# An RWKV scan followed by a soft mixture of experts: first loads on another queue, a split last weight, and a new order of all tasks

## The chip, the cores and the metric

The kernel runs on one core of a Trainium2 chip. The metric is the device time of one execution in microseconds (us), as the median of several runs. A profiled execution gives the times of the single instructions. In this text PE is TensorE, DVE VectorE, ACT ScalarE, POOL GpSimd and SP the engine that only issues transfers. A transfer is issued on the queue of one engine and is carried out by 16 DMA engines.

## What is computed

The reference is an RWKV-5 recurrence whose output goes through a soft mixture of experts:

```python
for t in range(S):                       # B=4, H=8, S=768, D=48
    cur = einsum('bhd,bhe->bhde', u * k[t], v[t])
    y[:, :, t] = einsum('bhd,bhde->bhe', r[t], state + cur)
    state = w * state + einsum('bhd,bhe->bhde', k[t], v[t])
x = y as (3072, 384)
logits = x @ phi                         # phi (384, 32): 8 experts of 4 slots
d = softmax of logits over the 3072 rows;  slot_input = d.T @ x
for e in range(8):                       # w1 (8, 384, 1024), w2 (8, 1024, 384)
    slot_out[e] = relu(slot_input[e] @ w1[e]) @ w2[e]
c = softmax of logits over the 32 slots;  out = c @ slot_out
```

The inputs k, r, v are 14.2 MB of f32, the weights w1 and w2 25.2 MB, the output 4.7 MB.

## The kernel before

The recurrence is cut into chunks of 128 times for two batches at once: 12 steps n, of which two share a load unit U (0 to 5). A unit has six loads (k, r, v for two batches x = 0, 1), each of 128 rows of 3072 bytes; the transfer casts f32 to bf16. They are issued on POOL (`load`, L333). For each unit PE transposes them (L447), DVE multiplies k and r by decay tables while it evicts (L458), ACT evicts v (L455). `pr` (L471, on POOL from unit 1 on) is the product of k and r. In step n PE turns k and v back (L485), forms A = k r (L512), which DVE masks (L517); it forms the state sums (L543, L547; evicted by ACT, L554; scaled to Z by POOL, L557) and y (L580 to L587), where DVE makes the diagonal term dv (L563). ACT evicts y to x (L594); x is transposed (L609, L612), and multiplied with phi (L628) into logits.

`combine(U)` makes the softmax over the slots (its last product on POOL, L664), `dispatch(g)` the slot inputs of four groups of steps, `finish_slots` folds them. `first_layer` (L863 to L889) has 4 experts side by side, each in 32 of the 128 output rows, for two groups g of four experts; its hidden units are transposed back (L886, L889) to hT. `second_layer` (L905) multiplies hT with w2: 64 products of 384 columns that all add into one bank `SO`, 4 experts side by side. One ACT instruction scales SO into `so` (L910). `output` forms 24 row groups of the output (L934), evicted in turn by DVE and ACT (L936, L938), and stores them by eight transfers of 1, 2, 3, 4, 4, 4, 4, 2 groups on SP (L940).

The weights are 16 transfers of 768 KB (as bf16) on POOL: w1 of 8 experts (L847), w2 of 8 experts (L850). w2 goes into the space that raw inputs had.

The order of the work is not that of the source. Every piece is a `task` with a priority, an engine, an estimated duration, what it reads and writes, and the buffers it uses. `Plan.order` simulates the engines, and chooses by time and by priority; the table TUNE shifts priorities of single tasks. `Plan.emit` then writes the instructions in that order, and puts filler matmuls on PE (L922) where the plan has gaps before the first A and after the last y. Each engine works strictly through its own list; waits for data are added by the framework. The list of POOL matters below: it holds pr, Z, the softmax products, and the issue of all transfers of inputs and weights.

At the start, DVE clears buffers, SP and ACT load w and u (four transfers of 1.5 KB, `wu`), SP loads phi, POOL issues k, and only then makes the identity matrix. PE clears eight banks (L387), and then transposes `wu` (L399), from which come the logarithms (L402) and the decay tables (L407, L410).

Of the kernel before, what the change touches and what calls it, by code (L numbers as in the profile page):

```python
# [11 lines left out]
class Plan:  # L12
# [4 lines left out]
    def __init__(self, tune):  # L17

        self.tune = tune
        self.tasks, self.pools, self.writers, self.readers, self.users = [], {}, {}, {}, {}  # L20
        self.slot, self.landed = {}, []
# [30 lines left out]
    def order(self):  # L52
# [9 lines left out]
        while ready:  # L62
            best = None
            for i in ready:
# [51 lines left out]
        return [i for _, _, i in sorted(out)]  # L116

    def emit(self, where, fill, took=0.22):
# [11 lines left out]
TUNE = {46: (0.6, 0.0), 47: (-0.81, 0.2), 48: (-0.47, 0.0), 49: (1.82, 0.0), 50: (-0.25, 0.2), 73: (-2.02, 0.0),   # L130
# [82 lines left out]
def kernel(  # L213
# [176 lines left out]
    for b_ in banks:  # L390
        task(-150, "PE", 0.4, lambda b_=b_: clear(b_), r=["warm"], w=["cleared"], n=1)
# [557 lines left out]
    for e in range(E):  # L949
        load_w(e, True)  # L950
# [41 lines left out]
```

## Time and profile before

| what | value |
|---|---|
| median of 3 runs | 119.11 us (118.87 to 119.14) |
| the profiled execution's own time | 118.71 us |
| its span, first to last instruction | 116.9 us |
| granted TensorE clock | 0.973 |
| busy: PE, DVE, ACT, POOL | 99.7, 92.9, 78.4, 72.6 us |
| HBM read, written | 39.38 MB, 4.72 MB |

How to read it: the profile's durations are of one profiled execution, whose own time is 1.8 us longer than its span. A row of the timeline gives start, duration (of the first start to the last end where there are several), engine, line, operation, output and input, and count; in brackets stands what the engine waited for before. PEld is the load of weights into the array. POOL's rows `DMA_DIRECT2D` are its time for issuing a transfer; SPq and ACTq are issues on those queues. A row of the stretches gives, after the stretch, its length, the busy time and the number of instructions of PE, PEld, DVE, ACT and POOL, the granted clock, the share of the DMA engines' time that was busy, and the GB/s that they wrote.

### The profile page before, as it was taken

The page shows a single profiled execution, that of the slowest core. Times are in us where ns is not written, and L with a number is a line of the kernel's source. Part 1 is how long each engine was busy: PE and PEld are TensorE (multiplying, and loading weights), DVE is VectorE, ACT ScalarE, POOL GpSimd, SP SyncE. Part 2 cuts the span into 40 slices and gives each one's busy share as a digit, 9 for nine tenths or more (in the row PEclk, how much of TensorE's full clock was granted, in tenths as well). Part 3 has the DMA queues.
Part 4 walks back from the last instruction along what each step waited for, and adds up shares of the span by engine and source line. Part 5 has one row for each costly group of instructions (what it writes and reads, how often), then busy time and mean ns, then how long its engine had stood idle before and what let it go on. Part 6 is the DMA issues. An engine that isn't in the chain of part 4 may idle for free.

```text
span 116.9 us, 4280 instructions
## 1 busy us (share of the span) xinstructions
PE 99.7 (85%) x1844; PEld 71.7 (61%) x1844; DVE 92.9 (80%) x152; ACT 78.4 (67%) x159; POOL 72.6 (62%) x111
## 2 busy tenths in 40 slices
PE   5979999999998999999989998999899995655200
PEld 1354587778786788777868777787665552445100
DVE  6789599999999999999999899999975561086400
ACT  4261878788789697895888898889764750175400
POOL 6999848999999999894769945999111010000000
PEclk9999999999999999999999999999999999999955
DMA  2999999999999999999999999999999994059994
GB/s 10 171 187 198 208 206 205 209 205 209 206 207 209 230 209 212 223 210 221 214 208 224 210 220 210 214 219 216 208 219 216 210 219 98 0 196 410 419 421 170
DMA packets 9122, 24.70 MB, mean 211 GB/s; under 512 B 1424, under 2 KB 6160, under 8 KB 9104
## 3 DMA queue, kind: packets, MB, share of 16 engines
q0 software_dynamic: 7488, 19.66, 87.2%
q1 hardware_dynamic: 1584, 4.77, 10.4%
q8 instruction: 14, 0.23, 0.7%
q14 instruction: 4, 0.03, 0.1%
q10 hardware_dynamic: 32, 0.00, 0.0%
HBM read 39.38 MB, written 4.72 MB: 377 GB/s over the span
## 4 chain that ended last, share of the span: by engine, by line
PE 32%; POOL 27%; DMA 24%; issue 4%; DVE 4%; ACT 2%; DVEq 0%; POOLq 0%
DMA raw<-in_moe_w_dram 17%; POOL raw L339 12%; PE T L447 8%; POOL arena L471 7%; DMA raw<-in_k_dram 7%; POOL Z L557 5%; PE T L485 5%; PE Ab L512 3%; DVE arena L936 3%; PE Y L580 2%; PE T L609 2%; ACT arena L938 2%; PE Y L587 1%; PE Sb L531 1%; PE Y L585 1%
## 5 line engine op out<-in xcount | busy, mean ns | idle before, releaser
L458 DVE TENSOR_TENSOR arena<-T,tab 128x1024 bf16<-128x1024 bf16 x24 | 29.0, 1217 | 2.5 <-PE T L447 2.2
L517 DVE TENSOR_TENSOR arena<-Ab,mask 128x1024 bf16<-128x1024 f32 x24 | 29.2, 1216 | 0.9 <-PE Ab L512 0.8
L447 PE MATMUL T<-by_head,raw 128*48 128x128 bf16 x576 | 22.8, 221 | 1.2 <-DMA raw<-in_r_dram 0.7
L471 POOL TENSOR_TENSOR arena<-arena 128x1024 bf16<-128x1024 bf16 x10 | 21.4, 2136 | 0.6 <-DVE arena L458 0.5
L447 PEld LDWEIGHTS <-raw 128*48 128x48 bf16 x576 | 16.9, 102 | 6.4 <-issue 3.3
L557 POOL TENSOR_TENSOR Z<-Ss,wCm 128x384 bf16<-128x384 f32 x20 | 16.7, 841 | 5.1 <-ACT Ss L554 5.0
L455 ACT COPY arena<-T 128x1024 bf16<-128x1024 bf16 x12 | 12.2, 1017 | 3.7 <-PE T L447 3.5
L594 ACT CAST x_all<-Y 128x384 bf16<-128x384 f32 x23 | 11.1, 489 | 1.6 <-PE Y L587 1.5
L485 PE MATMUL T<-ident,arena 112*128 112x112 bf16 x176 | 12.0, 213 | 0.1
L554 ACT COPY Ss<-Y 128x384 f32<-128x384 f32 x20 | 9.7, 491 | 3.0 <-PE Y L547 2.7
L563 DVE TENSOR_TENSOR dv<-vn,Sb 128x768 bf16<-128x768 bf16 x12 | 11.3, 946 | 0.2
L489 ACT COPY vn<-T 128x768 bf16<-128x768 bf16 x12 | 9.7, 811 | 2.4 <-PE T L485 2.2
L612 ACT COPY xT<-T 128x768 bf16<-128x768 bf16 (+2 forms) x13 | 9.7, 758 | 1.3 <-PE T L609 1.0
L485 PEld LDWEIGHTS <-arena 112*128 112x128 bf16 x176 | 9.3, 97 | 1.5 <-DVE arena L458 0.3
L512 PE MATMUL Ab<-arena 48*128 48x128 bf16 x192 | 9.7, 219 | 0.3 <-issue 0.3
L664 POOL TENSOR_TENSOR Le<-E,rs 128x128 bf16<-128x128 f32 x6 | 2.4, 400 | 11.5 <-PE Ab L863 5.9
L580 PE MATMUL Y<-vn,arena 128*128 128x48 bf16 x192 | 8.8, 184 | 0.2 <-DVE arena L517 0.2
L489 ACT COPY kn<-T 128x768 bf16<-128x768 bf16 x10 | 8.0, 805 | 0.8 <-PE T L485 0.7
L339 POOL DMA_DIRECT2D raw<-in_k_dram x12 | 6.5, 554 | 2.4 <-DMA raw<-in_v_dram 1.4
L587 PE MATMUL Y<-dv,ident 128*128 128x384 bf16 x24 | 7.8, 325 | 0.0
L580 PEld LDWEIGHTS <-arena 128*128 128x128 bf16 x192 | 6.8, 96 | 1.4 <-DVE arena L517 0.3
L512 PEld LDWEIGHTS <-arena 48*128 48x128 bf16 x192 | 5.5, 94 | 3.1 <-issue 1.6
(146 smaller groups left out, 197.9 us busy)
## 6 DMA issues: line engine op xcount, KB each, us to landing
w_all<-in_moe_w_dram POOLq DMA_DIRECT2D x8, 768.0 KB, 17.7
raw<-in_moe_w_dram POOLq DMA_DIRECT2D x8, 768.0 KB, 20.6
out_dram<-arena SPq DMA_DIRECT2D x4, 768.0 KB, 5.6
raw<-in_k_dram POOLq DMA_DIRECT2D x12, 192.0 KB, 6.9
raw<-in_r_dram POOLq DMA_DIRECT2D x12, 192.0 KB, 7.0
raw<-in_v_dram POOLq DMA_DIRECT2D x12, 192.0 KB, 7.2
out_dram<-arena SPq DMA_DIRECT2D x2, 384.0 KB, 2.4
out_dram<-arena SPq DMA_DIRECT2D x1, 576.0 KB, 2.9
```

The source lines that it names most:

```text
L339: pool.dma_start(out=raw_of(which, U, x), in_=ap)), w=[("raw", 6 * U + 2 * which + x)], dma=0.97, lag=7)
L447: O(pe.transpose(T[64 * x:64 * x + D, C * j:C * j + C], raw_of(which, U, x)[:, jj * D:(jj + 1) * D], by_head[:]))
L455: O(act.copy(dst, src))
L458: O(dve.tensor_mul(dst.rearrange("p j (h c) q -> p j h c q", c=2), src.rearrange("p j (h c) q -> p j h c q", c=2), tb[:, :, :, None, :].to ...
L471: O((pool if U else dve).tensor_mul(pr_t[P["pr", 2 * U + b]].rearrange("p (h a) -> p h a", h=H), kt, rt))
L485: O(pe.transpose(T[:, h * C:h * C + 64 + D], cell(st[P[src, U]], h, cc)[0:64 + D], ident[0:64 + D, 0:64 + D]))
L489: O(act.copy(nt[P[name, n]][:].rearrange("p h x d -> p (h x) d")[:, :, 0:D], T[:].rearrange("p (a d) -> p a d", d=64)[:, :, 0:D]))
L512: O(pe.matmul(Ab[:, x, i * C:(i + 1) * C], cell(kt, 4 * rd + i, cc)[s], cell(rt, 4 * rd + i, cc)[s], start=True, stop=True))
L517: O(dve.tensor_mul(AT[:, :, 4 * rd:4 * rd + 4, :], Ab[:].rearrange("p x (h t) -> p x h t", h=4), mask[:, None, None, :].to_broadcast([128, ...
L557: task(n + 0.2 + 0.05 * hh, "POOL", 0.8, lambda hh=hh: O(pool.tensor_mul(Z_t[P["Z", (n, hh)]][:], Ss_t[P["Ss", (n, hh)]][:], wCm[:, 4 * hh ...
L563: O(eng.tensor_mul(dv_t[P["dv", n]][:].rearrange("p h x d -> p (h x) d"), vn_t[P["vn", n]][:].rearrange("p h x d -> p (h x) d"), sums[:, : ...
L580: O(pe.matmul(Y[:, (2 * i + x) * D:(2 * i + x + 1) * D], AT[:, x, h, :], vn[:, h, x, :], start=(i == 0 and x == 0), stop=False, skip_group ...
```

## The change

- **First loads.** The two k transfers of unit 0 are issued on SP, as f32 without a cast, into the space of the AT ring; one ACT copy each casts them to bf16. w and u on SP follow the first of them, phi the second. POOL issues r first, and makes the identity between its first two loads.
- **phi.** phi is read as `(p mo) s` and not `(mo p) s`, so each of 128 rows is 384 bytes long and no longer three rows of 128 bytes. The transposition of x therefore takes every third column (`mi:Dm:nM`).
- **Clears.** Of the clears, the transposition of `wu` waits only for that of its own bank (in SEQ it comes fourth on PE, after three clears); two warm-up matmuls instead of six.
- **Last weight.** w2 of expert 7 comes in two transfers, of 6 and of 2 of its 8 row blocks y. The experts 3 and 7 (the last of each group) leave SO: they add into two banks of their own, halves of 192 columns. The scaling into `so` is three instructions: ACT for 96 rows of 384 columns, and, for the last 32 rows, ACT and DVE for 192 columns each.
- **Output.** Nine transfers of 1, 1, 1, 2, 3, 4, 4, 4, 4 groups. The first group is formed and evicted in two halves, by ACT and DVE.
- **Step 11.** The first part of its x transposed is evicted by DVE instead of ACT, and its transposition waits for all of x.
- **Order.** TUNE is gone. A list SEQ of all 613 tasks sets the order of every engine.

POOL's own list, from SEQ, in names (it holds no transfer outside this list but k of unit 0):

```
r U0 x0, identity, r U0 x1, identity, iota, v U0, k U1 x0, ucol, k U1 x1, r U1, v U1, k U2, ...
... w1 6, pr n6, pr n7, Z n6, Le U0, w1 7, Z n6, w2 0, phi4, w2 1, Z n7, pr n8, Ed U1, Z n7, pr n9,
w2 2, Z n8, Z n8, Ed U2, Z n9, pr n10, Z n9, Le U1, Le U2, pr n11, phi4, w2 3, Ed U3, w2 4, w2 5,
Z n10, Z n10, phi4, w2 6, Le U3, Le U4, Le U5, w2 7 (6 blocks), w2 7 (2 blocks)
```

PE's list ends, after the last transposition of x and the slot inputs, with the first layer, then

```
hT g0 b1, hT g0 b0, h g1 a0, rest 0 x1, hT g1 b0, hT g1 b1,
most 0, rest 0 x0, most 1, most 2, most 3, rest 1 x0, rest 1 x1, rest 2 x1, rest 2 x0
```

DVE's list around the end of the recurrence is: ev r U5 b1, dv n9, AT n9, rs U1, rs U2 and their reciprocals, AT n10, dv n10, AT n10, rm U3, cm g1, AT n11, dv n11, AT n11 (ev is L458, AT L517).

```diff
-    def __init__(self, tune):
-        self.tune = tune
+    def __init__(self, tune, seq=()):
+        self.tune, self.seq = tune, seq
...
-            for i in ready:
+            if self.seq:
+                i = self.seq[len(out)]
...
+            for i in () if self.seq else ready:
...
-        return [i for _, _, i in sorted(out)]
+        return list(self.seq) or [i for _, _, i in sorted(out)]
...
+        if i == 0:
+            for x in (at,):
+                st = AT_t[x].bitcast(f32)[:, 0:JD]
+                task(-220, "SP", 1.7 - 0.8 * x, lambda x=x, st=st: O(sp.dma_start(out=st, in_=aps[x])), r=["sp"], w=[("st", x), "sp"])
+                task(-98, "ACT", 0.75, lambda x=x, st=st: O(act.copy(raw_of(0, 0, x), st)), r=[("st", x)], w=[("raw", x)])
...
-    banks = [t[:].bitcast(f32) for t in T_b] + [Ab[:, 0, :], Ab[:, 1, :], Y_b[0][:], Y_b[1][:], Sb[:]]
+    banks = [Sb[:]] + [t[:].bitcast(f32) for t in T_b] + [Ab[:, 0, :], Ab[:, 1, :], Y_b[0][:], Y_b[1][:]]
...
-    warm_up(6, -94, r=["cleared"])
+    warm_up(2, -94, r=["cleared1"])
...
-                        O(pe.transpose(T[:, o:o + C], xx[:, x, mi * C:(mi + 1) * C], ident[:]))
+                        O(pe.transpose(T[:, o:o + C], xx[:, x, mi:Dm:nM], ident[:]))
...
+            y0, y1 = (0, nF) if e < E - 1 else (YL if part else 0, nF if part else YL)
+            more = dict(w=[("w2", e, 1)], behind=w2_first[e]) if part else dict(
+                w=[("w2", e, 0)] + [("raw", 4 * e + i) for i in range(4)])
+            w2_first.setdefault(e, task(-40 + e + 10 * part, "POOL", 0.57, lambda: O(pool.dma_start(
+                out=w2_of(e)[:, y0:y1], in_=moe_w2[e].rearrange("(p y) d -> p y d", p=128)[:, y0:y1])),
+                dma=3.7 * (y1 - y0) / nF, lag=lag, **more))
...
+        lk = [("Y", "so0"), ("Y", "so1")]
+        EL, DH, RL = EG - 1, Dm // 2, 32 * (EG - 1)
+        def most(g, y0, y1):
+            for y in range(y0, y1):
+                for j in range(EL):
+                    O(pe.matmul(SO[32 * j:32 * j + 32, :], hT[g][:, y, 32 * j:32 * j + 32], w2_of(g * EG + j)[:, y, :],
+                                start=(g == 0 and y == 0), stop=(g == 1 and y == nF - 1), skip_group_check=True))
+        def rest(g, y0, y1, x):
+            s = slice(x * DH, (x + 1) * DH)
+            for y in range(y0, y1):
+                O(pe.matmul(Y_b[P[lk[x]]][RL:128, 0:DH], hT[g][:, y, RL:128], w2_of(g * EG + EL)[:, y, s],
+                            start=(g == 0 and y == 0), stop=(g == 1 and y == nF - 1), skip_group_check=True))
+        for q, (g, y0, y1) in enumerate(((0, 0, YH), (0, YH, nF), (1, 0, YH), (1, YH, nF))):
...
+        for q, (g, y0, y1) in enumerate(((0, 0, nF), (1, 0, YL), (1, YL, nF))):
...
+        task(80, "ACT", 0.55, lambda: O(act.mul(so[0:RL, :], SO[0:RL, :], rcs[0:RL, 0:1])), r=["SO", "rcs"], w=["so"], use=key)
+        task(81, "ACT", 0.35, lambda: O(act.mul(so[RL:128, 0:DH], Y_b[P[lk[0]]][RL:128, 0:DH], rcs[RL:128, 0:1])),
...
+        task(81, "DVE", 0.35, lambda: O(dve.tensor_scalar(
+            out=so[RL:128, DH:Dm], in0=Y_b[P[lk[1]]][RL:128, 0:DH], scalar1=rcs[RL:128, 0:1], scalar2=None, op0=ALU.mult)),
...
-        for sz in (1, 2, 3, 4, 4, 4, 4, 2):
+        for sz in (1, 1, 1, 2, 3, 4, 4, 4, 4):
...
+                for x, cp in enumerate((act.copy, dve.tensor_copy)):
+                    s = slice(x * Dm // 2, (x + 1) * Dm // 2)
+                    O(pe.matmul(ob[x][:, s], LexpT[:, 0:Nn:nN], so[:, s], start=True, stop=True))
+                    O(cp(obuf[:, 0, s], ob[x][:, s]))
```

More of the change, by code (lines that the diff above doesn't have):

```diff
@@ L63, in order @@
             best = None
-            for i in ready:
+            if self.seq:
+                i = self.seq[len(out)]
+                assert not wait[i]
+                eng, use = tasks[i][1], tasks[i][5]
+                at = max(since[i], free.get(eng, 0.0))
+                need = [k[0] for k in use if k not in self.slot]
+                for k in need:
+                    got = sorted(f for f in self.pools[k] if f is not None)
+                    at = max(at, got[need.count(k) - 1])
+                best = (at, 0.0, i, at)
+            for i in () if self.seq else ready:
                 prio, eng, _, _, _, use, _, _ = tasks[i]
@@ L128, in emit @@
             self.tasks[i][3]()
-TUNE = {46: (0.6, 0.0), 47: (-0.81, 0.2), 48: (-0.47, 0.0), 49: (1.82, 0.0), 50: (-0.25, 0.2), 73: (-2.02, 0.0),
[78 rows of a table removed]
+TUNE = {}
+SEQ = [13, 0, 57, 11, 14, 12, 15, 63, 1, 64, 7, 6, 60, 102, 58, 54, 55, 89, 59, 73, 67, 61, 56, 65, 104, 66, 2, 4, 5,
[26 rows of a table added]
 @with_exitstack
@@ L294 @@
     MO = LO + 2 * ES
-    P = Plan(TUNE)
+    P = Plan(TUNE, SEQ)
     task = P.task
@@ L331, with load @@
     P.pool("E", 2)
-    def load(U, which):
+    def load(U, which, at=0):
         src = (k, r, v)[which]
         p, n = divmod(U, nU)
-        for x in range(2):
-            ap = src[2 * p + x, :, n * U2:(n + 1) * U2, :].rearrange("h (p j) d -> p h (j d)", j=J)
-            task(-101 if (U, which) == (0, 0) else -100 + U, "POOL", 0.54, lambda x=x, ap=ap: O(
-                pool.dma_start(out=raw_of(which, U, x), in_=ap)), w=[("raw", 6 * U + 2 * which + x)], dma=0.97, lag=7)
+        i = 6 * U + 2 * which
+        aps = [src[2 * p + x, :, n * U2:(n + 1) * U2, :].rearrange("h (p j) d -> p h (j d)", j=J) for x in range(2)]
+        if i == 0:
[3 more added lines that the diff above has]
+                task(-98, "ACT", 0.75, lambda x=x, st=st: O(act.copy(raw_of(0, 0, x), st)), r=[("st", x)], w=[("raw", x)])
+        else:
+            for x in range(2):
+                task(-100 + U, "POOL", 0.54, lambda x=x: O(pool.dma_start(out=raw_of(which, U, x), in_=aps[x])), w=[("raw", i + x)],
+                     dma=0.97, lag=7)
     O(act.preload_act_table_set("natural_log_exp_and_others"))
@@ L551, in step @@
             zr = [zin(hh)] if c > 0 else []
-            task(n + 0.1 + 0.05 * hh, "PE", 0.36 if c > 0 else 0.2, s_fn, r=[("kn", n), ("vn", n), "ident"] + zr,
+            task(n + 0.1 + 0.05 * hh, "PE", 0.36 if c > 0 else 0.2, s_fn, r=[("kn", n), ("vn", n), "ident", "cleared1"] + zr,
                  w=[("Ssp", n, hh)], n=5 if c > 0 else 4, use=[key, ("kn", n), ("vn", n)] + zr)
@@ L841, with load_w @@
     so = sb("so", [128, Dm], bf)
-    FH, PH, YH = F // 2, C // 2, nF // 2
-    def load_w(e, second):
+    FH, PH, YH, YL = F // 2, C // 2, nF // 2, nF - 2
+    w2_first = {}
+    def load_w(e, second, part=0):
         lag = 7 if not second and e < 3 else 5
@@ L849, in load_w @@
         else:
-            task(-40 + e, "POOL", 0.57, lambda: O(pool.dma_start(
-                out=w2_of(e), in_=moe_w2[e].rearrange("(p y) d -> p y d", p=128))),
-                w=[("w2", e)] + [("raw", 4 * e + i) for i in range(4)], dma=3.7, lag=lag)
+            y0, y1 = (0, nF) if e < E - 1 else (YL if part else 0, nF if part else YL)
[4 more added lines that the diff above has]
+                dma=3.7 * (y1 - y0) / nF, lag=lag, **more))
     def first_layer():
@@ L898, in second_layer @@
         key = [("S", "so")]
+        lk = [("Y", "so0"), ("Y", "so1")]
         begins = None
-        for g in range(2):
-            for a in range(2):
-                def mm(g=g, a=a):
-                    for y in range(a * YH, (a + 1) * YH):
-                        for j in range(EG):
-                            O(pe.matmul(SO[32 * j:32 * j + 32, :], hT[g][:, y, 32 * j:32 * j + 32], w2_of(g * EG + j)[:, y, :],
-                                        start=(g == 0 and y == 0), stop=(g == 1 and y == nF - 1), skip_group_check=True))
-                i = task(60 + 2 * g + a, "PE", 0.7, mm, r=[("hT", g, a)] + [("w2", g * EG + j) for j in range(EG)], w=["SO"],
-                         use=key, n=16)
-                begins = i if begins is None else begins
@@ new lines, in rest @@
+        def rest(g, y0, y1, x):
[4 more added lines that the diff above has]
+        for q, (g, y0, y1) in enumerate(((0, 0, YH), (0, YH, nF), (1, 0, YH), (1, YH, nF))):
+            i = task(60 + q, "PE", 0.04 + 0.165 * (y1 - y0), lambda g=g, y0=y0, y1=y1: most(g, y0, y1),
+                     r=[("hT", g, int(y0 >= YH))] + [("w2", g * EG + j, 0) for j in range(EL)], w=["SO"], use=key, n=EL * (y1 - y0))
+            begins = i if begins is None else begins
@@ new lines, in second_layer @@
+        for q, (g, y0, y1) in enumerate(((0, 0, nF), (1, 0, YL), (1, YL, nF))):
+            for x in range(2):
+                task(61.5 + q + 2 * (q > 0) + 0.1 * x, "PE", 0.03 + 0.083 * (y1 - y0), lambda g=g, y0=y0, y1=y1, x=x: rest(g, y0, y1, x),
+                     r=[("hT", g, a) for a in range(2)] + [("w2", g * EG + EL, int(q == 2))], w=[("SOl", x)], use=[lk[x]], n=y1 - y0)
+        task(80, "ACT", 0.55, lambda: O(act.mul(so[0:RL, :], SO[0:RL, :], rcs[0:RL, 0:1])), r=["SO", "rcs"], w=["so"], use=key)
@@ L929, in output @@
         i = 0
-        for sz in (1, 2, 3, 4, 4, 4, 4, 2):
+        for sz in (1, 1, 1, 2, 3, 4, 4, 4, 4):
             i0 = i
-            for _ in range(sz):
-                op = ob[i % 7][:, 0:Dm]
+            if i == 0:
+                for x, cp in enumerate((act.copy, dve.tensor_copy)):
+                    s = slice(x * Dm // 2, (x + 1) * Dm // 2)
+                    O(pe.matmul(ob[x][:, s], LexpT[:, 0:Nn:nN], so[:, s], start=True, stop=True))
+                    O(cp(obuf[:, 0, s], ob[x][:, s]))
+                i = 1
+            for _ in range(sz if i0 else 0):
+                op = ob[(i + 1) % 7][:, 0:Dm]
                 O(pe.matmul(op, LexpT[:, i:Nn:nN], so[:], start=True, stop=True))
@@ L950 @@
         load_w(e, True)
+    load_w(E - 1, True, 1)
     for U in range(UU - 2):
```

38 lines of the change are left out of this document (20 added, 18 removed), and 104 rows, old and new, of tables (SEQ, TUNE).

## The prediction

> **What bounds the kernel now.** I read the slices first, then the chain of waits in order of time, then fine stretches at both ends, then the timeline of each engine.
>
> ```profile
> DMA  2999999999999999999999999999999994059994
> GB/s 10 171 187 198 208 206 205 209 205 209 206 207 209 230 209 212 223 210 221 214 208 224 210 220 210 214 219 216 208 219 216 210 219 98 0 196 410 419 421 170
> 2.50:3.00 0.50, 0.50 (x2) 0.15 (x1) 0.47 (x4) 0.00 (x0) 0.50 (x4) 1.00 1.33 46
> 3.00:3.50 0.50, 0.50 (x3) 0.22 (x2) 0.50 (x6) 0.17 (x2) 0.50 (x3) 1.00 0.30 46
> 3.50:4.00 0.50, 0.50 (x3) 0.22 (x2) 0.47 (x5) 0.17 (x2) 0.50 (x2) 1.00 1.01 184
> ```
>
> The DMA engines are full from the second slice until the weights are in; then come a gap of about two slices and the output. The stream of inputs starts at 3.5 us: before that only small transfers run.
>
> ```profile
> 80.06 19.59 DMA raw<-in_moe_w_dram
> ...
> 99.69 1.46 PE L905 MATMUL Sb<-raw,tab 128*32 128x384 bf16 x29 [1.55 <-DMA raw<-in_moe_w_dram]
> ...
> 101.19 0.59 ACT so L910
> ...
> 101.82 0.50 PE T L934 x2
> ...
> 102.25 1.02 DVE L936 COPY arena<-T 128x384 f32<-128x384 f32 x2 [5.01 <-PE T L934]
> 102.83 8.01 SPq L940 DMA_DIRECT2D out_dram<-arena  x8
> ```
>
> The last w2 lands at 80.06 + 19.59 = 99.65. PE has waited 1.6 us for it, does 29 products, ACT scales, PE forms the first output group, DVE evicts it, SP issues at 102.83: 3.18 us after the landing. From that issue to the end of the span are 116.9 - 102.83 = 14.07 us, in which the stores run at about 410 GB/s. So the end is set by **landing + 3.18 + 14.07**.
>
> ```profile
> 7.87:83.05 75.18, 72.23 (x1556) 56.39 (x1556) 71.92 (x82) 60.49 (x114) 64.58 (x89) 1.00 1.09 212
> 7.87 1.22 DVE L458 TENSOR_TENSOR arena<-T,tab 128x1024 bf16<-128x1024 bf16 x1 [0.43 <-PE T L447]
> 61.02 2.34 DVE L458 TENSOR_TENSOR arena<-T,tab 128x1024 bf16<-128x1024 bf16 x2
> 81.83 1.22 DVE L517 TENSOR_TENSOR arena<-Ab,mask 128x1024 bf16<-128x1024 f32 x1
> 91.26 1.48 PE L863 MATMUL Y<-w_all,uns 128*32 128x512 bf16 x24
> 96.38 0.40 PE L886 MATMUL T<-ident,tab 128*128 128x128 bf16 x4
> ```
>
> The second limit is close behind. From its first eviction (7.87) to its last mask product (81.83 + 1.22 = 83.05) DVE is busy 71.92 of 75.18 us; PE is at 72.23. The first layer starts at 91.26, the last hidden transposition ends at 96.78, 2.9 us ahead of the landing. A change must move both, the stream and this chain.
>
> **The change, part by part.**
>
> Start of the stream.
>
> ```profile
> 1.02 0.40 SPq L344 DMA_DIRECT2D wu<-in_w_dram  x1
> 1.26 1.25 POOL L339 DMA_DIRECT2D raw<-in_k_dram  x2 [0.81 <-POOLq L976]
> DMA to landing us min/median/max: 3.8/7.0/8.7
> 103.50:104.00 0.50, 0.50 (x5) 0.46 (x4) 0.39 (x1) 0.23 (x1) 0.00 (x0) 1.00 0.57 203
> 5.94 0.78 PE L447 MATMUL T<-by_head,raw 128*48 128x128 bf16 x16
> ```
>
> POOL issues k at 1.26 and traffic begins at 3.5, 2.2 us later. SP issues an output at 102.83, and the half microsecond from 103.5 has a share of 0.57, so traffic begins near 103.7, 0.9 us later. SP waited for a DVE memset before 1.02; k needs none, so I put its issue at 0.8 and its traffic at 1.7. Two f32 loads of 393 KB at the output's 410 GB/s take 1.9 us and end at 3.6, when POOL's r, still issued at 1.26, arrives. So the stream starts 1.8 us earlier. The bytes read stay the same, but phi, which ran ahead of the stream (2.5 to 3.5, at shares of 1.33 and 0.30, so 0.8 us at most, with short rows), now runs inside it; its 48 KB alone are 0.1 us, and as its rows are longer now I take that. **Stream: -1.7 us** (bounds -0.5, if SP gains only its earlier issue, and -2.2). If all stays fed, the last landing is 97.95. POOL's own list has a wait early, ucol behind the first k of unit 1, which needs wu; POOL reaches it at about 5, after six issues, and wu is there by 4.1.
>
> The Trainium skill weighs against this: "DMA: Bandwidth & Descriptors", "Issuing engines are not separate DMA queues", says that all queues run on the same 16 engines and that issuing from several only saves issue time; its table gives a first byte after about 1 us from POOL and 0.6 from SP. By it the step would be worth an estimated 0.9 us (0.4, and 0.46 of earlier issue). The trace's 2.2 against 0.9 us disagrees; an outcome of that kind is a rival below.
>
> Start of the chain.
>
> ```profile
> 4.81 0.23 PE L399 MATMUL Sb<-ident_f,wu 16*128 16x16 f32 x1
> 5.29 0.21 ACT L402 ACTIVATE lnw<-wuT 128x8 f32<-128x8 f32 x1 [1.61 <-DVE wuT L401]
> L410 ACT ACTIVATE tab<-tab,biasP 128x512 f32<-128x512 f32 x4 | 2.7, 714 | 0.5 <-DVE tab L407 0.5
> out_dram<-arena SPq DMA_DIRECT2D x1, 192.0 KB, 1.9
> L489 ACT COPY vn<-T 128x768 bf16<-128x768 bf16 x12 | 9.7, 811 | 2.4 <-PE T L485 2.2
> ```
>
> The transposition of wu ran at 4.81 behind eight clears. Now three precede it, and w and u set it: the shortest SP landing is 1.9 us, k's 1 us of traffic may stand ahead, so 3.1 to 4.1; I take 3.6. The logarithm follows 0.48 later. ACT then casts the second k (0.81, by the row of a 128x768 copy; the first cast hides under the wait for wu), then 0.71 of exponential: DVE's first eviction at 3.6 + 0.48 + 0.21 + 0.81 + 0.71 = 5.8, with a hop 5.9 (5.3 to 7.0). That is **2.0 us earlier** than 7.87. PE's first transposition, 5.94, moves to about 5.1.
>
> The middle. Between these points DVE has 71.92 us of work; phi's copies, one memset and a table move in, 0.5 us. SEQ can save only idle time: 75.18 - 71.92 = 3.26 us. I give it 2.6 us idle afterwards (0 to 6; nearest to what is there): DVE's last mask product ends at 5.9 + 72.4 + 2.6 = 80.9, **2.15 us earlier** (call it g). The tail from there to the first layer, 91.26 - 83.05 = 8.2 us, is a chain of latencies with the same operations; SEQ only reorders it, and I keep 8.2. In it the first part of step 11's x moves from ACT to DVE and waits for all of x: at most the 0.37 us that a 128x256 copy takes on ACT (row below), hidden behind ACT's larger second part; zero.
>
> ```profile
> L609 PEld LDWEIGHTS <-x_all 128*128 128x128 bf16 x72 | 4.3, 97 | 1.2 <-ACT x_all L594 0.2
> L823 PEld LDWEIGHTS <-accb 128*128 128x128 bf16 x3 | 0.2, 103 | 0.2
> ```
>
> Loading every third column costs 103 ns (L823 does so already) against 97: 72 loads, 0.4 us, hidden behind matmuls of 0.22 us. Zero.
>
> The second layer.
>
> ```profile
> L905 PE MATMUL Sb<-raw,tab 128*32 128x384 bf16 x64 | 3.5, 328 | 1.6 <-DMA raw<-in_moe_w_dram 1.6
> 43.38 0.17 PE Y L547 x4
> ```
>
> Four experts side by side overlap: 29 products in 1.46 us, of which 0.33 is the last one's own time, are 40 ns apart, 160 ns for four. With three the row stays 160 ns: 16 rows, 2.6 us. The fourth runs alone: L547's four products of 96 columns in 0.17 us make 43 ns each, so 192 columns 83 ns, and 32 of them 2.65 us. The layer doubles, from 2.6 to 5.2 us of PE. And most of it now follows the last hidden transposition: most 0 to 3 (4 x 0.66), rest 0 x0 (0.66), rest 1 (2 x 0.5), 4.3 us. In the old trace that transposition ends at 96.78; with a bank wait less and one rest part ahead of it I leave it there. So PE reaches the last four products at 96.78 + 4.3 - g = **101.1 - g**, and I take 100.9, since part of most 0 can run in the shadow of the last eviction. With g = 2.15 that is 98.75, later than the landing of 97.95. PE, not the weight, now ends last.
>
> POOL's list.
>
> ```profile
> 53.36 0.59 POOL L850 DMA_DIRECT2D raw<-in_moe_w_dram  x1
> 64.45 0.59 POOL L850 DMA_DIRECT2D raw<-in_moe_w_dram  x1
> 77.98 2.12 POOL L471 TENSOR_TENSOR arena<-arena 128x1024 bf16<-128x1024 bf16 x1
> 94.13 0.40 POOL L664 TENSOR_TENSOR Le<-E,rs 128x128 bf16<-128x128 f32 x1 [5.89 <-PE Ab L863]
> raw<-in_moe_w_dram POOLq DMA_DIRECT2D x8, 768.0 KB, 20.6
> L563 DVE TENSOR_TENSOR dv<-vn,Sb 128x768 bf16<-128x768 bf16 x12 | 11.3, 946 | 0.2
> ```
>
> w2 3, issued at 64.45, now stands behind pr n11, and w2 7 behind the softmax product of unit 5 (94.13). pr n10 can start when DVE has evicted the last r. After that eviction DVE's list holds three dv (0.9), five mask products (1.13 apart, as the pair of evictions that takes 2.34 us shows) and 1.65 of small ones until 83.05 - g, so it ends at 73.0 - g. POOL then needs 2.12 + 0.8 + 2 x 0.4 + 2.12 + 0.3 with hops 6.3: w2 3 is issued at **79.3 - g**. An empty queue needs 2.8 us (3.8 of the first k less its own 1.0) besides the transfer, and a w2 takes about 3.7 (eight landings from 53.36 + 20.6 to 99.65). w2 3 to 7 then end at 79.3 - g + 2.8 + 5 x 3.7 = **100.6 - g** at the earliest: 98.45, hardly above 97.95. w2 7 needs issue by about 91.4; unit 5's product moves ahead of the first layer's evictions in DVE's list, some 90. Covered, as long as g holds.
>
> After the landing.
>
> ```profile
> L612 ACT COPY xT<-T 128x256 bf16<-128x256 bf16 x1 | 0.4, 372 | 0.2 <-PE T L609 0.2
> L936 DVE COPY arena<-T 128x384 f32<-128x384 f32 x6 | 3.1, 549 | 5.0 <-PE T L934 5.0
> ```
>
> Four products of 192 columns: 0.45 with latency. Half scalings side by side: 0.37 and a hop. First half group: 0.35 until evicted from (as 101.82 to 102.25, less columns), half copies 0.33, hops 0.15. Together **1.65** for 3.18. The stores afterwards move the same bytes; one issue more, 0.33 us of SP, hides under 0.47 us per group. 14.07 stays.
>
> Sum: last four products at 98.75, first store at 100.4 (before: 102.83), so the span is 116.9 - 2.4 = 114.5, the profiled execution 116.3 (1.8 around it, as now), and the median, which lies 0.4 above the profiled time now, **116.7**.
>
> **Rivals.**
>
> 1. DVE's idle time nearly vanishes (g over 3): the landing, 97.95, ends last. First store 99.6, median 115.9. For: early stretches starve for loads that now come sooner. Against: only 3.26 us are there.
> 2. SP saves only issue time: its k takes POOL's 3.8 us from issue to landing. Then the stream starts 0.46 earlier (0.8 against 1.26), the two k land at 4.6 and 5.6, cast (0.81) and transposition (0.6) put DVE's first eviction at 7.0, g = 1.05, the last products at 99.85, the first store at 101.5, the median at 117.8. For it speaks that w and u, from SP at 1.02, let PE start no earlier than 4.81; against it the output's 0.9 us.
> 3. **Slower**: the order costs DVE idle time. Both w2 3 on POOL (100.6 - g) and PE's doubled second layer (100.9 - g) follow g one for one. The new kernel loses when these pass 99.69 + 3.14 - 1.65 = 101.2, that is g below -0.3: DVE's last mask product after 83.35, some 5 us of idle. At g = -1 the first store goes at 103.55 and the median is 119.8. For: transfers that were issued 15 us ahead hang on computed products. Against: DVE's start alone gives 2 us.
>
> **How the numbers follow.** Forecast (g 1.2 to 3, median 115.9 to 117.6) 0.62; rival 1 0.10; rival 2 0.14; rival 3 0.10; between 2 and 3 the rest, 0.04. The range goes from 115.0 (rival 1 with the stream's bound of -2.2, and 0.4 less after the landing) to 118.7 (g = 0.15). A measurement here tells 0.3% (0.36 us): faster 0.86, same 0.05, slower 0.09.
>
> **What would show it.** DMA share near 1 from about 1.7 us; first eviction near 5.9; last mask product near 80.9; no low DMA share between 78 and 92; last products near 98.7, first store 1.65 later. Wrong would be a hole in the DMA share after w2 2, or a first eviction after 7.

## The result, and the profile after

The changed kernel takes 125.06 us (median of 4 runs, 124.67 to 125.21) against 119.12 (118.87 to 119.48) beside it: ratio 1.049, interval 1.045 to 1.053. It is slower by 6 us; 116.7 was forecast. Its profiled execution took 125.12 us with a span of 123.3. Some executions of a kernel take over 1.5% longer than its fastest one; the medians and ratios below leave them out.

The slices of the page after, DMA share and GB/s:

```profile
DMA  2999999799959999999999999999999998149993
GB/s 31 243 250 207 207 211 203 143 144 148 136 98 160 181 216 215 217 217 217 211 217 215 211 217 219 211 215 201 203 211 217 215 211 173 18 154 402 411 417 149
```

Two things are to be seen. The second and third slice carry more than before (243 and 250 against 171 and 187), partly because the stream starts earlier. And from the eighth to the fourteenth slice (21 to 43 us) it runs at 98 to 181 GB/s, where it ran at 205 to 230 before. Later slices are about as before; what is lost between 21 and 43 us never comes back.

Stretches of the kernel before, and then of the one after (last columns: clock, DMA share, GB/s):

```profile
0.00:20.00 20.00, 17.86 (x262) 10.49 (x263) 16.46 (x43) 11.35 (x20) 16.04 (x42) 1.00 0.99 168
20.00:44.00 24.00, 23.51 (x526) 18.70 (x524) 23.82 (x25) 19.52 (x35) 23.77 (x34) 1.00 1.14 210
44.00:80.00 36.00, 34.61 (x771) 27.81 (x769) 34.32 (x44) 30.94 (x63) 29.27 (x31) 1.00 1.04 215
80.00:96.00 16.00, 15.62 (x218) 9.56 (x218) 11.98 (x30) 10.73 (x31) 3.52 (x7) 1.00 1.04 215
```
```profile
0.00:20.00 20.00, 14.55 (x162) 8.25 (x164) 12.22 (x34) 8.51 (x13) 12.51 (x34) 1.00 1.00 192
20.00:44.00 24.00, 23.09 (x526) 18.46 (x523) 23.73 (x26) 19.18 (x34) 20.22 (x27) 1.00 0.92 150
44.00:80.00 36.00, 34.46 (x772) 27.82 (x769) 35.09 (x43) 29.69 (x61) 28.79 (x33) 1.00 1.05 215
```

The GB/s count what is written, and a k that arrives as f32 writes 0.39 MB more for the two transfers. Without them the first 20 us carry 172 GB/s, not 192: the stream is 0.08 MB, **0.4 us, ahead** at 20 us. The next 24 us carry 60 GB/s less, 1.44 MB or 6.8 us at 210 GB/s. So it is 6.4 us late from 44 us on, and at the end 7.1: the last landing is at 106.75 (the smaller part of w2 7, issued at 96.45, 10.3 us to landing) instead of 99.65.

The first microseconds, on SP's own timeline, then for all engines:

```profile
0.74 0.65 SPq L302 DMA_DIRECT2D arena<-in_k_dram  x1
1.45 0.51 SPq L313 DMA_DIRECT2D wu<-in_w_dram  x1
2.02 0.28 SPq L314 DMA_DIRECT2D wu<-in_u_dram  x1
2.33 0.55 SPq L302 DMA_DIRECT2D arena<-in_k_dram  x1
```
```profile
4.98 0.83 ACT L303 CAST raw<-arena 128x768 bf16<-128x768 f32 x1 [2.96 <-DMA arena<-in_k_dram]
...
6.01 0.25 PE L368 MATMUL Sb<-ident_f,wu 16*128 16x16 f32 x1 [2.62 <-DMA wu<-in_u_dram]
...
8.97 0.83 ACT L303 CAST raw<-arena 128x768 bf16<-128x768 f32 x1 [2.25 <-DMA arena<-in_k_dram]
...
11.01 1.23 DVE L427 TENSOR_TENSOR arena<-T,tab 128x1024 bf16<-128x1024 bf16 x1 [2.32 <-PE T L416]
```

The first k lands at 4.94, 4.2 us after its issue; w and u let PE start at 6.01; the second k lands at 8.94, 6.6 us after its issue. The first eviction follows at 11.01, where 5.9 was forecast and 7.87 is what the old kernel has.

What that does to the stream, from the groups of lines (before, then after) and from POOL's timeline:

```profile
L557 POOL TENSOR_TENSOR Z<-Ss,wCm 128x384 bf16<-128x384 f32 x20 | 16.7, 841 | 5.1 <-ACT Ss L554 5.0
L526 POOL TENSOR_TENSOR Z<-Ss,wCm 128x384 bf16<-128x384 f32 x20 | 16.8, 840 | 10.9 <-ACT Ss L523 10.9
```
```profile
22.89 0.83 POOL L526 TENSOR_TENSOR Z<-Ss,wCm 128x384 bf16<-128x384 f32 x1 [4.48 <-ACT Ss L523]
23.67 0.56 POOL L306 DMA_DIRECT2D raw<-in_r_dram  x1
24.22 1.05 POOL L306 DMA_DIRECT2D raw<-in_v_dram  x2
```

POOL stands 4.48 us before the first Z, whose input hangs on the late chain, and the loads that its list has behind that Z are issued when the queue has run dry. The old kernel's first Z starts at 18.86, without a wait. The two holes in the stream:

```profile
24.00:26.00 2.00, 1.85 (x40) 1.36 (x39) 2.00 (x3) 2.00 (x4) 1.67 (x4) 1.00 0.47 49
36.00:38.00 2.00, 1.31 (x31) 0.93 (x28) 2.00 (x3) 1.54 (x3) 2.00 (x5) 1.00 0.40 39
```

The first follows that wait. Ahead of the second POOL issues no load between 32.31 and 35.70 us, since it runs a product of k and r (2.16 us) and a Z; order_alone below has the same hole without the late chain.

The end of the chain of waits:

```profile
95.47 0.40 POOL Le L633
95.87 0.04 issue
95.91 9.92 DMA raw<-in_moe_w_dram
105.83 0.04 issue
105.88 1.50 PE Y L888 x16
107.37 0.02 issue
107.39 0.42 ACT so L900
```

The first store goes at 108.77, 2.02 us behind the last landing (before: 3.18; forecast 1.65). From there to the end are 14.53 us, 0.46 more than before: 7.1 - 1.16 + 0.46 = 6.4, the difference of the two spans.

### The profile page after: what moved, and what is told of

Read it like the earlier page. It is cut to its first block, busy times and chain, and to the rows that moved or that the text cites. A ratio compares the mean times of both kernels' runs of the same rounds, so it can differ in the third digit from the quotient of the medians.

```text
span 123.3 us, 4309 instructions
## 1 busy us (share of the span) xinstructions
PE 101.6 (82%) x1847; PEld 74.4 (60%) x1847; DVE 93.9 (76%) x154; ACT 79.4 (64%) x162; POOL 71.3 (58%) x110
## 4 chain that ended last, share of the span: by engine, by line
PE 45%; DMA 13%; POOL 10%; DVE 10%; ACT 10%; issue 4%; SPq 1%; DVEq 0%; POOLq 0%
PE T L416 11%; DMA raw<-in_moe_w_dram 8%; DMA arena<-in_k_dram 5%; POOL raw L306 4%; PE Ab L481 4%; PE T L454 4%; POOL arena L440 3%; PE Y L549 3%; DVE arena L937 3%; DVE arena L486 3%; PE Y L916 3%; PE T L578 2%; PE Y L556 2%; POOL Z L526 2%; PE Y L554 2%
## 5 line engine op out<-in xcount | busy, mean ns | idle before, releaser
L416 PE MATMUL T<-by_head,raw 128*48 128x128 bf16 x576 | 23.9, 231 | 1.3 <-ACT raw L303 1.3
L416 PEld LDWEIGHTS <-raw 128*48 128x48 bf16 x576 | 18.2, 108 | 6.7 <-issue 3.6
L458 ACT COPY vn<-T 128x768 bf16<-128x768 bf16 x12 | 9.7, 812 | 3.1 <-PE T L454 3.1
L581 ACT COPY xT<-T 128x768 bf16<-128x768 bf16 (+1 forms) x12 | 9.3, 784 | 0.4 <-PE T L578 0.4
L458 ACT COPY kn<-T 128x768 bf16<-128x768 bf16 x10 | 8.1, 814 | 0.6 <-PE T L454 0.6
L306 POOL DMA_DIRECT2D raw<-in_r_dram x12 | 6.7, 557 | 1.7 <-DMA raw<-in_k_dram 0.8
L516 PE MATMUL Y<-vn,kn 128*128 128x96 bf16 x80 | 6.7, 206 | 0.1
```

The source lines that it names most:

```text
L306: task(-100 + U, "POOL", 0.54, lambda x=x: O(pool.dma_start(out=raw_of(which, U, x), in_=aps[x])), w=[("raw", i + x)], dma=0.97, lag=7)
L416: O(pe.transpose(T[64 * x:64 * x + D, C * j:C * j + C], raw_of(which, U, x)[:, jj * D:(jj + 1) * D], by_head[:]))
L458: O(act.copy(nt[P[name, n]][:].rearrange("p h x d -> p (h x) d")[:, :, 0:D], T[:].rearrange("p (a d) -> p a d", d=64)[:, :, 0:D]))
```

## The experiments

Theory A: SP's first loads make the loss. Theory B: the new order does, by itself. Theory C: the doubled second layer eats what the split weight gains. Each ratio is to the kernel before on the same chip, with its interval.

**old_order**: all edits, but the tasks in the old order.

```diff
-SEQ = [13, 0, 57, 11, ...
+SEQ = [2, 0, 11, 1, ...
```

The two k and their casts stand in front, the new rests where their weights land.

> All edits of the change, but the tasks in the order of the kernel before (new tasks put beside those they belong to). Theory A, the first loads: k of unit 0 through SP still lands at 5 and 9 us and w and u near 6, so the first eviction on DVE stays near 11 instead of 7.9 and the time stays 2 to 4 us above the kernel before, 121 to 123. Theory B, the new order itself is what costs: with the old order the time falls to 118 or less, since the tail after the last weight is 1.2 us shorter.

Measured 121.93 us, 1.020 (1.010 to 1.030). A holds for the time, but the first eviction is later still, at 13.36, and the reason is new. Its timeline of all engines:

```profile
10.08 0.83 ACT L303 CAST raw<-arena 128x768 bf16<-128x768 f32 x1 [4.26 <-DMA arena<-in_k_dram]
...
11.09 0.18 POOL L389 COPY wCm<-wC 64x8 f32<-64x8 f32 x1 [4.92 <-ACT wC L385]
...
11.28 0.36 DVE L400 CAST phi<-phi_f 128x32 bf16<-128x32 f32 x3 [5.70 <-DMA phi_f<-in_moe_phi_dram]
```

phi, behind k on SP, lands 8.3 us after its issue, and DVE waits 5.7 us for it; ACT stands before the cast of the second k, and wC behind that cast holds up POOL and its loads for 4.9 us. Three engines wait, each in its own order, behind something that SP delivers late.

**order_alone**: the code of before, the tasks in the order of SEQ.

> The kernel before with nothing changed but the order of its tasks, which is that of the new list (the two k loads first on POOL, the bank clears in their old place). Theory A: the chain starts near 8 to 9 us, POOL's first Z comes by 20, no hole in the DMA share of the loads, and the time is 118 to 120. Theory B: holes between 24 and 38 us as in the changed kernel, and 122 to 125.

Measured 122.95, 1.029 (1.021 to 1.037): B holds as well, with k on POOL and the first eviction at 7.71. Its stretches show where, against 210, 215 and 215 GB/s before:

```profile
20.00:44.00 24.00, 23.11 (x517) 18.48 (x516) 23.86 (x26) 19.32 (x35) 23.38 (x32) 1.00 1.07 191
44.00:80.00 36.00, 34.01 (x753) 27.15 (x751) 34.61 (x43) 29.26 (x60) 28.02 (x32) 1.00 1.04 215
80.00:96.00 16.00, 16.00 (x231) 9.81 (x228) 13.10 (x36) 12.32 (x39) 6.28 (x13) 1.00 1.01 195
```

24 x 19 = 0.46 MB, 2.2 us, are lost between 20 and 44 us, 16 x 20 = 0.32 MB, 1.5 us, between 80 and 96. Together 3.7: the last w2 lands at 92.85 + 10.45 = 103.30 instead of 99.65. POOL's timeline shows the first of the two holes made:

```profile
28.58 0.53 POOL L299 DMA_DIRECT2D raw<-in_v_dram  x1
29.10 2.17 POOL L431 TENSOR_TENSOR arena<-arena 128x1024 bf16<-128x1024 bf16 x1
31.19 0.86 POOL L517 TENSOR_TENSOR Z<-Ss,wCm 128x384 bf16<-128x384 f32 x1
31.96 0.56 POOL L299 DMA_DIRECT2D raw<-in_v_dram  x1
```

For 2.9 us no load is issued, and the stretch from 32 to 34 us moves 44 GB/s. The second hole stands where w2 3 is issued at 80.12 instead of 64.45.

**k_on_pool**: the changed kernel with k of unit 0 on POOL, with cast, first in its list.

```diff
-            for x in (at,):
...
-                task(-220, "SP", 1.7 - 0.8 * x, lambda x=x, st=st: O(sp.dma_start(out=st, in_=aps[x])), r=["sp"], w=[("st", x), "sp"])
-                task(-98, "ACT", 0.75, lambda x=x, st=st: O(act.copy(raw_of(0, 0, x), st)), r=[("st", x)], w=[("raw", x)])
...
+        for x in range(2):
+            task(-100 + U, "POOL", 0.54, lambda x=x: O(pool.dma_start(out=raw_of(which, U, x), in_=aps[x])), w=[("raw", i + x)],
```

> The changed kernel, with k of unit 0 loaded as before: by POOL, with the cast in the transfer, first in POOL's list; w and u then have the SP queue for themselves. Everything else, the order too, as in the changed kernel. Theory A: w and u land before 4, the first eviction is near 7 to 8 and the time 117 to 119.5, so that more than 5 of the 6 us come back. Theory B: under 2 us come back, 123 or more.

Measured 121.69, 1.018 (1.004 to 1.033): between the two. About 3.4 of the 6 us come back, so neither theory is enough. Its last weight lands at 102.8.

**tail_only**: the kernel before with the split w2 7, the two banks and the output groups, in the old order.

> The kernel before, in its old order, with the last weight in two transfers, experts 3 and 7 in banks of their own and the new output groups: nothing else of the change. Theories A and B: the tail from the last landing to the first store is 2.0 instead of 3.2 us, PE is done before that landing, so 117.7 to 118.2. Theory C, the doubled second layer costs what the split saves: PE reaches the last products after the landing and the time is 119 or more.

Measured 118.08, 0.989 (0.983 to 0.996): **faster than both kernels**. First store at 101.66 instead of 102.83. C falls for this order.

What made the order slow? In order_alone POOL's list as built differs from SEQ: the fourth fill of sumI, which SEQ has behind a load of unit 5, ran at 19 us, and the product of step 3 ran seven places early (the 2.17 us above). The helper that ties each instruction to the one before it leaves the register move of such a fill free, and what hangs behind it could move up; that this is how it happened is inferred.

**order_kept**: order_alone with that fill behind the third, so that the list stays as SEQ has it.

In names:

```diff
-... Z n2, r U5 x1, sumI#4, pr n3, v U5 ...
+... sumI#3, sumI#4, ... Z n2, r U5 x1, pr n3, v U5 ...
```

> The kernel before with the new order, and one task put earlier in POOL's list: the fourth fill of sumI right behind the third. In the runs with the new order POOL did not work its list off as written: that fill ran at about 19 us instead of behind a load of unit 5, and a product of 2.16 us (that of step 3) with it ran ahead of five loads; the stream of inputs then lost 2.1 us between 30 and 38 us. With the fill early the list stays as written. Theory L (the slipped product opens the hole): no low DMA share between 30 and 38, the stream 1.4 us behind the old kernel's at the end (the late weights of the second layer are still there) instead of 3.5; 120.9 (120.3 to 121.4). Rival O (the new order costs by itself, because the first Z stands later and its loads behind it): the hole stays, 122.5 to 123.2.

Measured 123.35, 1.035 (1.021 to 1.049). L falls: the stretch from 32 to 34 us is at 185 GB/s instead of 44, but those from 38 to 42 are at 157 and 180, so the hole only moved. Its timeline shows a new wait ahead of it:

```profile
32.84 2.60 DVE L391 CAST phi<-phi_f 128x32 bf16<-128x32 f32 x1
...
33.25 2.14 POOL L431 TENSOR_TENSOR arena<-arena 128x1024 bf16<-128x1024 bf16 x1
...
35.49 0.25 PE L588 MATMUL Sb<-phi,xT 128*128 128x32 bf16 x4 [2.07 <-DVE phi L391]
```

SEQ puts phi's three casts between the products. One that takes 0.17 us elsewhere takes 2.60 here, to the end of POOL's product, and PE waits 2.07 us for it. And the weights of the first layer still stand behind 8 to 17 Z and products, where they stood behind 7 to 14.

**order_kept_w2**: w2 3 to 7 earlier as well.

> As order_kept, and the last five weights of the second layer are issued earlier in POOL's list (after 24 to 30 of the products and Z instead of 28 to 30 and the last softmax product). Theory L with W (the late issue of these weights opens a second hole of 1.4 us at 80 to 86): no hole is left, the last landing is that of the old kernel within 0.5 us and the time 119.2 (118.6 to 119.8). Rival O: 121 to 122, with a stream that is 2 us behind from 36 us on. If the compute chain of the new order is shorter, nothing is gained beyond the old kernel's time, since the landing sets the end.

Measured 120.8, 1.012 (1.000 to 1.024): the earlier weights bring back most of it, but the time lies between the two theories and the interval is wide.

**after_kept**: the changed kernel with the fill moved.

> The kernel after the change with the fourth fill of sumI right behind the third, so that POOL's list stays as written. Theory L: the part of the stream that is lost from 32 to 38 us comes back (the loads of unit 5 no longer stand behind the product of 2.16 us), 122.6 to 123.4; what the late first eviction loses at 22 to 28 us (some 2 us) stays. Rival S (all of the loss hangs on the late start: the loads wait for Z products whose inputs are late, whatever stands between them): 124.5 to 125.3.

Measured 125.74, 1.054 (1.042 to 1.067): no gain, and the same stall of a phi cast (2.60 us, at 37.03). S is nearer, though the time lies above its range.

**fed**: the kernel before with the order of SEQ on PE, DVE and ACT; in POOL's list (in names) the last loads and all weights forward.

```diff
-... r U5 x1, pr n3, v U5, Z n2, w1 0, pr n4, Z n3, w1 1, ...
+... r U5 x1, v U5, w1 0, pr n3, w1 1, w1 2, Z n2, w1 3, pr n4, w1 4, ...
-... pr n9, w2 2, ..., pr n11, phi4, w2 3, Ed U3, w2 4, w2 5, ..., Le U5, w2 7
+... pr n8, w2 2, ..., pr n9, w2 3, ..., w2 4, ..., pr n10, w2 5, ..., w2 6, pr n11, w2 7
```

> The kernel before with the new order on PE, DVE and ACT, and in POOL's list the loads of unit 5 and the weights of both layers moved forward, so that each stands behind as many Z and products as in the old list. Keeping the list as written had only moved the hole: the first-layer weights still stood behind 8 to 17 products and the stream was 2.5 us behind at 56. Theory F (the new order costs because POOL's list feeds the stream late; the order of the computation is free): the stream stays within 0.5 us of the old kernel's all along, the last landing is at 99.7 to 100.2 and the time 119.3 (118.7 to 119.9). Rival O (the computation itself is slower in the new order, Z n0 0 and all behind it later): the landing comes early, PE reaches the last products later than it, 120.5 or more.

Measured 120.04, 1.010 (1.007 to 1.014); the stretch from 20 to 44 us is at 207 GB/s and the last w2 lands at 100.31. Both lie 0.1 past F's ranges, so F holds for the larger part: two thirds of what the order cost was POOL's list. The computation itself gains nothing: from the first eviction (7.66) to the end of the last mask product (83.01) are 75.35 us, 75.18 before.

**fed_k**: k_on_pool with the same list. **after_fed**: the changed kernel with it, and six loads ahead of the first Z.

> The kernel after the change with k of unit 0 loaded by POOL, first in its list, and the repair of the list: the split of the last weight, phi's rows and the new order stay. Theory F: 118.2 (117.6 to 118.7), as the split alone. Rival O: 119.5 or more. If the new order's computation is shorter behind an undisturbed stream, it cannot show here, since the landing ends last.

> The kernel after the change with the same repair of POOL's list, and six loads put ahead of the first Z, which waits 4.5 us there. The stream should stay the 2 us ahead that it gains at its start, last landing about 98. What is left is the late first eviction (11.0 instead of 7.9). Theory C (that lateness goes through the whole chain: last mask product near 86.8, and PE reaches the last products 17.6 to 18.8 us behind it): last products at 104.4 to 105.6, 122.3 to 123.5. Rival D (the chain has slack behind the stream, and all that was lost was stream): 117 to 119.

Measured 119.59, 1.005 (1.002 to 1.009), and 123.4, 1.035 (1.026 to 1.045). F of fed_k falls, since the time is its rival's: with POOL's list repaired SEQ's order still costs about 1%. C of after_fed holds, but not the stream: it runs at 183 GB/s from 20 to 44 us, and the last weight lands at 102.8, not near 98. PE's last products wait for no weight any more. The last mask product on DVE and the last products on PE, of fed_k and of after_fed:

```profile
83.00 1.23 DVE L478 TENSOR_TENSOR arena<-Ab,mask 128x1024 bf16<-128x1024 f32 x1
...
101.48 0.99 PE L880 MATMUL Y<-raw,tab 128*32 128x192 bf16 x10
```
```profile
85.39 1.23 DVE L486 TENSOR_TENSOR arena<-Ab,mask 128x1024 bf16<-128x1024 f32 x1
...
103.84 0.99 PE L888 MATMUL Y<-raw,tab 128*32 128x192 bf16 x10
```

PE ends 18.2 us behind the last mask product in both (102.47 - 84.23, 104.83 - 86.62). So the changed kernel has two limits past the old end: the landing, and, with POOL's list repaired, this chain. In fed_k, where k comes from POOL, the chain from the first eviction (7.52) is the longer part: 76.7 us, in one profiled execution, against 75.2 before.

**old_order_k**: k_on_pool with the tasks in the old order.

> The kernel after the change with the tasks in the order of before and k of unit 0 loaded by POOL: only the split with its banks, phi's rows, the strided weights and the fewer clears stay. If SP's loads of k are all that the old order suffers from, it loses the 3.8 us that they cost there: 118.0 (117.5 to 118.5). If phi's rows or the clears cost something: 119 or more, as against 118.1 of the split alone.

Measured 118.3, 0.993 (0.988 to 0.997), not to be told from the split alone. So phi's rows, the strided weights and the fewer clears are worth nothing that shows, and SP's k costs 2.8% in the old order (1.020 against 0.993).

**k_alone**: after_kept with POOL's first load behind the product that waits for w and u. Seen once.

> As after_kept, but POOL issues its first load behind the product that waits for w and u, so that SP's two f32 loads of k and the small ones have the 16 DMA engines to themselves. Theory S1 (SP's loads are slow because they share the engines with POOL's loads): k 0 lands within 3 us of its issue at 0.74, w and u by 4, the second k by 5 (issued at 2.3), DVE's first eviction at 6.5 to 7.5, though the stream starts some 3 us later. Rival S2 (f32 loads of k, 128 rows of 3 KB from 8 heads, are slow by themselves, or a queue of SP works them off one after the other): the second k lands at 8 or later still, first eviction after 10.

Landings of k on SP in the changed kernel, then in this one, min, median, max:

```profile
DMA to landing us min/median/max: 4.2/5.4/6.6
```
```profile
DMA to landing us min/median/max: 4.1/4.3/4.6
```

S1 holds by half. With the engines to itself the second k takes 4.6 us instead of 6.6: the 2.0 us are POOL's loads. But the first takes 4.1 anyway, no less than POOL's own k (3.8 at the shortest), w and u let PE start at 5.72 and not by 4, and the first eviction is at 9.10, still later than with k on POOL (125.66 us, since the stream starts late).

**k1_next**: after_fed, the second k issued on SP right behind the first. **k1_next_old**: the same in the old order, with wC ahead of the second cast, phi's casts behind the first evictions and their copies behind the loads of unit 2.

> As after_fed (the change with POOL's list repaired), and SP issues the second f32 load of k right behind the first, ahead of w and u: at about 1.4 instead of 2.33. Theory Q (it was late because of its place behind w and u): it lands by 6.5, the first eviction is at 8.5 to 9.3, set by w and u, and since PE's chain ends last in after_fed the time falls by as much, to 121.3 to 122.2. Theory E (it shares the engines with POOL's queued loads wherever it stands): it lands at 8 or later, the first eviction stays at 10.3 or later and the time at 123 to 124.

> All edits with the tasks in the old order, the second k right behind the first on SP, and three things moved so that nothing waits behind them: wC on ACT ahead of the second cast (POOL's loads had waited 5 us behind it), phi's copies on DVE behind the first evictions (DVE had waited 5.7 us there), their copies on POOL behind the loads of unit 2. Theory Q: first eviction at 8.5 to 9.3, the stream 1.5 to 2 us ahead, and PE, which ends last with the split second layer, ends some 0.7 to 1.4 later than with k on POOL: 118.8 to 119.8. Theory E: first eviction 10.3 or later, 120.3 to 121.5. If SP's start were a gain at all, it would be under 118.1, the time of the split alone.

Measured 123.15, 1.035 (1.027 to 1.043), and 121.7, 1.021 (1.011 to 1.032, from two executions). E has the times, within 0.2 us for the second, but not the whole mechanism. All engines of k1_next:

```profile
8.11 0.26 PE L368 MATMUL Sb<-ident_f,wu 16*128 16x16 f32 x1 [3.01 <-DMA wu<-in_u_dram]
...
11.50 1.22 DVE L427 TENSOR_TENSOR arena<-T,tab 128x1024 bf16<-128x1024 bf16 x1 [0.70 <-PE T L416]
```

Now the second k lands 5.8 us after an issue before 2.0, ahead of E's 8, and w and u, 1.5 KB each and issued by 2.9, hold PE until 8.11 (7.40 in k1_next_old). The wait changed its owner: in both arrangements, of k, w and u, what SP issues last is late.

Step by step, with PE or the stream ending last: the split, 0.989; with the other edits, 0.993; with SEQ's computation and a fed list, 1.005; with SP's k, 1.035; with SEQ's own list, 1.049. So SP's k costs about 3%, SEQ's list about 1.4% and SEQ's computation about 1.2%. The landing alone shows how they add: 99.65 before, 102.8 with either SP's k (after_fed) or SEQ's list (k_on_pool), 106.75 with both.

## Why the prediction was wrong

**The step that failed is the start of the stream**: "Two f32 loads of 393 KB at the output's 410 GB/s take 1.9 us and end at 3.6", with w and u at 3.6 beside them. They landed at 4.94 and 8.94, and w and u let PE start at 6.01. Traffic did begin early, near 2.0 us instead of 3.5, but in its first microsecond it ran at 93 and 74 GB/s, and then below 410:

```profile
2.00:2.50 0.50, 0.50 (x3) 0.21 (x2) 0.44 (x6) 0.02 (x1) 0.50 (x2) 1.00 0.94 93
2.50:3.00 0.50, 0.50 (x3) 0.00 (x0) 0.42 (x3) 0.00 (x0) 0.43 (x3) 1.00 0.46 74
3.00:3.50 0.50, 0.39 (x1) 0.00 (x0) 0.44 (x4) 0.00 (x0) 0.50 (x2) 1.00 0.79 313
3.50:4.00 0.50, 0.00 (x0) 0.00 (x0) 0.33 (x2) 0.00 (x0) 0.50 (x2) 1.00 1.07 345
```

By 4.0 us 0.41 MB were written, one k's worth, where two were to be in by 3.6; the stream gained 0.4 us of the 1.7. Why the first microsecond is slow stays open. What was left out: the second k stood behind w and u on SP, at 2.33; a load of k brings about 4 us from issue to landing on either queue (3.8 the shortest on POOL, 3.7 to 4.2 the first on SP in the runs); and POOL's loads, queued by then, share the engines. The Trainium skill ("DMA: Bandwidth & Descriptors", "Issuing engines are not separate DMA queues") says that transfers of all engines interleave on the same 16 and only issue time is saved; k_alone (4.6 against 6.6 us) agrees with the first half, and the 0.4 us are nearer to the 0.9 that the rule gave than to 1.7.

The second step that failed is **"If all stays fed"**. The last landing was forecast at 97.95 and came at 106.75, 8.8 us later: 1.3 are the start that was not gained, 6.8 were lost between 20 and 44 us, 0.7 at the end. The loads of units 4 and 5 and the first-layer weights stand behind products and Z in POOL's list, and what makes these late was not worked out; k_on_pool and after_fed show that the late start and the list each cost the landing some 3 us.

- **Start of the chain**: forecast 5.9, measured 11.01, past the 7 that was named as a sign of being wrong. Rival 2 had k at 4.6 and 5.6; the first was right, the second 3.3 us short.
- **Idle time of DVE**: 2.6 us given. The row below, of the stretch from its first eviction to just past the end of its last mask product (86.77), has 75.99 - 72.86 = 3.1. Right; g = 83.05 - 86.77 = -3.7 comes from the start.

```profile
11.01:87.00 75.99, 73.47 (x1564) 57.59 (x1561) 72.86 (x84) 59.39 (x113) 60.85 (x84) 1.00 1.02 193
```

- **Second layer**: PE at the last four products at 100.9 - g. after_fed (g = -3.6) gives 104.5 for 104.4 measured, fed_k (-1.2) 102.1 for 102.0. Right.
- **POOL's list**: w2 3 at 79.3 - g = 83.0; measured as in the row below (in order_alone, with g = -0.7, 80.0 for 80.12). Right as far as it went: the loads ahead of w2 3 were the hole in it.

```profile
83.11 0.58 POOL L825 DMA_DIRECT2D raw<-in_moe_w_dram  x1
```

- **Strided weights**: 105 ns against 97, hidden. Right.
- **After the landing**: 2.02 for 1.65. The last products end 0.61 us after the landing (0.45 forecast); the rest lies in the scaling and the half copies, of which DVE's starts 0.18 behind ACT's. The 14.07 us became 14.53, and not through the stores: in the old order this part takes 13.9 to 14.1 us in all five profiles, with the old stores and the new, and the quickest store lands in 1.9; in SEQ's order, with its variants, it takes 14.4 to 14.8 in all eleven, and the quickest store lands in 2.7 to 3.2. What in the order does that stays open.
- **Rival 3** had half of it: both ends follow g one for one with the turn at -0.3. With the measured g of -3.7 its sum gives a first store at 106.3 and a median of 122.5; after_fed has 106.25 and 123.4. The other 2.5 us to the changed kernel's 108.77 are the starved stream, which it did not have. It was priced at 0.10 because idle time in the middle was to cause it, not a late start.

## What to carry to other kernels

In a kernel that its input stream bounds, count for each load how many products stand ahead of it in the issuing engine's list: whatever makes these products late empties the queue, and here the loss was never made up. Moving a first load to another engine gains only if its landing, not its issue, comes earlier; ask what else is queued by then, and which engines wait in order behind what it delivers. An edit worth a per cent (here the split weight) can be lost in a bundle; run it alone.

## What was not expected of the hardware

- A DVE cast of 128 x 32 from f32 took 2.60 us instead of 0.17 while POOL issued a load and ran a product of 2.14 us, and ended with it. The same cast took 2.60 to 2.62 in all four runs in which that product stands where SEQ's list has it. In the changed kernel two casts took 0.44 and 0.95. The Trainium skill ("GPSIMD Engine Reference", "1. Specifications") has POOL's interfaces to SBUF shared with VectorE, with contention for some of its instructions; these rows agree: the casts were held, while a mask product beside such a product of POOL kept its 1.22 us.
- Transfers of 1.5 KB (w and u), issued on SP by 2.9 us behind two of 393 KB, let PE start at 8.11 only. The trace shows PE's wait for u, not the landing of the single transfers.
- With two f32 loads in place of two with cast the DMA engines were as busy in the first 20 us (share 1.00 against 0.99), though they wrote 0.39 MB more for the two.
- The quickest store landed 1.9 us after its issue in all five profiles in the old order, and 2.7 to 3.2 in all eleven in SEQ's.
